# Token-tile attention and channel mix on one core: batch-wise pipeline on 64-token tiles, quarter-tile matmuls and a searched issue order

## The chip, the core, the metric

The kernel runs on one core of a Trainium2 chip. The metric is the device time of one execution in microseconds (us). Executions of one kernel differ (those of before beside the change took 107.15 to 110.02 us), so every run carries a state: "fast", or "slow" when it took over 1.5% more than the fastest of its kernel. Verdicts use fast runs alone. A median that is quoted is over all runs. A ratio is the mean time of one kernel's fast runs over the mean of the other's fast runs of the same rounds on the same chip, so it is not quite the ratio of the medians; the interval beside it covers 95%.

The engines are called as in the profile: PE is TensorE's matmul (PEld its weight load), DVE is VectorE, ACT is ScalarE, POOL is GpSimd, SP is SyncE.

## The reference

```python
# q, k, v: (4 batches, 4 heads, 1088 tokens, 32); S1, S2: (8, 32); all float32
def phi(x):                                   # 64 features for every token and head
    a = einsum('rd,bhsd->bhsr', S1, x)
    b = einsum('rd,bhsd->bhsr', S2, x)
    return einsum('bhsi,bhsj->bhsij', a, b).reshape(*x.shape[:-1], 64)
q_p, k_p = phi(q), phi(k)
kv  = einsum('bhsf,bhsd->bhfd', k_p, v)       # sum over all tokens of a batch
z   = k_p.sum(axis=2)
x   = (q_p @ kv) / (q_p @ z + 1e-6)           # then heads side by side: (4, 1088, 128)
# channel mix, d_ff = 1024
x_prev = x shifted by one token
xk = mu_k * x + (1 - mu_k) * x_prev
xr = mu_r * x + (1 - mu_r) * x_prev
out = sigmoid(xr @ w_r) * (maximum(xk @ w_k, 0) ** 2 @ w_v)
```

Denominators can come close to zero, so the attention half has to stay in float32. The channel mix (the "MLP" below) is done in bf16.

## The kernel before

It works on two batches at a time. A tile is 128 rows: 64 tokens of one batch and 64 of the other. k and q arrive partly head-major and partly token-major; the token-major half is turned by TensorE. In its trace each float32 matmul of the program stands as two passes (the 34 matmuls of the k projection, L198, as 68 records), and each pass as two instructions on TensorE, a weight load and a matmul (1,375 and 1,365 records in all).

```python
    def k_proj(half, gi):                     # per tile one matmul on the full array: 128 rows x 64 columns
        ...
            nc.tensor.matmul(p[:, t * 64:t * 64 + 64], kT[half][:, t0 + t, :], SW[:, 0, :, :2, :], skip_group_check=True)

    def k_acc(half, gi):                      # already in quarter tiles: 64 rows x 64 columns each
        ...
                    nc.tensor.matmul(kv[hp:hp + 64, b2, (h // 2) * 64:(h // 2) * 64 + 64],
                                     f[rows, t - t0, h].rearrange("p i j -> p (i j)"),
                                     _ap(rhs, [[(H - h) * NT * D, 2], [1, D]]), ...
                                     tile_position=(64 * b2, hp))

    def q_proj(g):                            # per tile two half-width matmuls, 96 columns each
        ...
                nc.tensor.matmul(p[64 * b2:64 * b2 + 64, t * 96:t * 96 + 96], qT[half][:, T, 64 * b2:64 * b2 + 64],
                                 SW[:, 2 * half + b2].rearrange("p h x r -> p (h x r)"), ...
                                 tile_position=(0, 64 * b2))

    def mm1(g, cp):                           # first MLP matmul of a group of tokens
        ...
    # loads: k0, v0, k1, q0, v1, q1 on three queues, and on GpSimd the weights only behind the second v pair:
    nc.gpsimd.tensor_copy(warm[:], tok["v1"][:R, 0, 0, :1])
    nc.gpsimd.dma_start(mu_k[:], moe_mu_k.rearrange("d -> d ()"))
    nc.gpsimd.dma_start(wk[:, :, :2 * P], moe_w_k.rearrange("p (c f) -> p c f", c=4))
```

The order in which tasks are issued is worked out by a small list scheduler with keys in the program. Zero matmuls ("fillers", 128x512) keep TensorE busy at the start: 19 of them, 7.6 us of busy time before 10.4 us (L84).

## Time and profile before

| | before |
|---|---|
| median, beside the change | 108.06 us (107.15 to 110.02, 4 runs) |
| profiled span | 107.7 us |
| first and last MLP matmul (mm1) | 52.1 and 102.5 us |
| instructions on TensorE (matmuls and weight loads) | about 2,750 |

The profile of before fell in a slow run (109.86 us, mean granted clock 0.95).

These are lines of the page of the kernel before. "busy us (share) xinstructions" comes first; then the span in 40 slices of 2.7 us, one digit each, in tenths; the queue that brings instructions; and the shares of the chain that ended last.

```profile
PE 95.0 (88%) x1365; PEld 71.6 (66%) x1375; DVE 77.8 (72%) x160; ACT 70.3 (65%) x124; POOL 10.6 (10%) x33
...
PE   5999990598789999976999999999999999999850
...
DVE  3275690123549796949999998599997997878770
ACT  0500410830293533767699999989999998999940
...
PEclk9999999679955699999999999999999999999999
...
q8 instruction: 11, 0.18, 0.7%
...
PE 50%; DMA 19%; ACT 13%; issue 5%; POOL 4%; DVE 3%; SPq 3%; ACTq 0%; POOLq 0%
```

The second half of the span is full on three engines; the first half is not. The table of stretches of the same kernel gives the figures (stretch, its length, then busy us of each engine with the instructions, the granted clock, the DMA share and GB/s), and the view of the mm1 line shows where the dense part begins (minimum/median/maximum duration, first and last start).

```profile
0.00:30.00 30.00, 23.75 (x368) 17.22 (x368) 13.78 (x35) 7.45 (x17) 8.30 (x21) 0.94 0.89 236
30.00:52.00 22.00, 20.31 (x411) 17.52 (x413) 17.21 (x37) 12.44 (x30) 2.31 (x13) 0.85 0.12 14
52.00:102.00 50.00, 49.03 (x568) 35.73 (x577) 44.71 (x85) 48.84 (x75) 0.00 (x0) 1.00 0.11 38
...
L398 PE MATMUL h<-XK,wk x62: 269/379/390, 52.1 to 102.5; 128*128 128x512 bf16 x54, 128*128 128x256 bf16 x8
```

### The profile page before, as it was taken

What the parts mean: (1) busy time and instruction counts of PE and PEld (TensorE: products, weight loads), DVE (VectorE), ACT (ScalarE), POOL (GpSimd) and SP (SyncE); (2) the same over time, 40 slices, a digit from 0 to 9 for tenths busy, and PEclk for the clock granted to TensorE, in tenths of its full rate; (3) what the DMA queues carried; (4) which work ended last, traced back from release to release, by engine and by line L of the source; (5) the groups of instructions that cost most, each with busy time, mean ns of one, the idle gap of its engine ahead of it and who ended that gap; (6) DMA issues with size and microseconds to landing.
All of it is one profiled execution on the core that took longest, in us unless ns stands there. A gap on an engine that the chain in (4) does not pass through costs nothing.

```text
span 107.7 us, 3217 instructions
## 1 busy us (share of the span) xinstructions
PE 95.0 (88%) x1365; PEld 71.6 (66%) x1375; DVE 77.8 (72%) x160; ACT 70.3 (65%) x124; POOL 10.6 (10%) x33
## 2 busy tenths in 40 slices
PE   5999990598789999976999999999999999999850
PEld 2445990487679889754667687776866776677720
DVE  3275690123549796949999998599997997878770
ACT  0500410830293533767699999989999998999940
POOL 7050000007790000000000000000000000000000
PEclk9999999679955699999999999999999999999999
DMA  0999999994990000000000000200202002122221
GB/s 10 343 293 366 279 280 287 209 272 159 127 98 0 0 6 6 3 6 0 3 0 6 0 0 0 97 6 0 97 6 97 0 8 90 30 73 97 97 100 53
DMA packets 6157, 9.70 MB, mean 90 GB/s; under 512 B 1520, under 2 KB 2416, under 8 KB 6144
## 3 DMA queue, kind: packets, MB, share of 16 engines
q1 hardware_dynamic: 3360, 6.13, 18.9%
q0 software_dynamic: 1952, 1.71, 8.7%
q10 hardware_dynamic: 832, 1.67, 4.9%
q8 instruction: 11, 0.18, 0.7%
q14 instruction: 2, 0.02, 0.1%
HBM read 7.80 MB, written 2.23 MB: 93 GB/s over the span
## 4 chain that ended last, share of the span: by engine, by line
PE 50%; DMA 19%; ACT 13%; issue 5%; POOL 4%; DVE 3%; SPq 3%; ACTq 0%; POOLq 0%
DMA tok_v_67<-in_v_dram 19%; PE o L419 10%; PE h L398 8%; PE xps L361 8%; PE qtp L323 7%; PE abwp L294 7%; PE tp L187 3%; PE kv L227 3%; PE abp L198 2%; SPq L71 2%; ACT r L435 1%; ACT PP_179 L379 1%; DVE osb L440 1%; ACT k_1507 L404 1%; PE rps L427 1%
## 5 line engine op out<-in xcount | busy, mean ns | idle before, releaser
L398 PE MATMUL h<-XK,wk 128*128 128x512 bf16 (+1 forms) x62 | 17.6, 366 | 0.2
L206 DVE TENSOR_TENSOR kp<-ab 128x1024 f32<-128x1024 f32 (+1 forms) x10 | 10.4, 1060 | 6.5 <-ACT ab L168 6.5
L187 PE MATMUL tp<-ident,tall 128*128 128x128 f32 x34 | 6.9, 340 | 4.1 <-ACT tall L182 4.1
L323 PE MATMUL qtp<-ident,qp 128*128 128x128 f32 x68 | 9.4, 275 | 1.1 <-ACT abw L168 1.0
L206 DVE TENSOR_TENSOR qp<-abw,an 128x1024 f32<-128x1024 f32 (+1 forms) x9 | 10.3, 1154 | 0.0
L168 ACT COPY qpT<-qtp 128x512 f32<-128x512 f32 x15 | 8.3, 601 | 2.4 <-PE qtp L323 2.3
L361 PE MATMUL xps<-qpT,kvbd 128*64 128x256 f32 (+3 forms) x80 | 9.3, 358 | 0.5 <-ACT qpT L168 0.5
L84 PE MATMUL zps<-zero 128*128 128x512 bf16 x19 | 7.6, 578 | 1.3 <-POOL zero L79 1.3
L323 PEld LDWEIGHTS qtp<-ident,qp 128*128 128x128 f32 x68 | 7.4, 142 | 1.6 <-ACT abw L168 1.2
L168 ACT COPY ab<-abp 128x256 f32<-128x256 f32 (+1 forms) x8 | 2.8, 352 | 8.8 <-PE abp L198 8.7
L187 PEld LDWEIGHTS tp<-ident,tall 128*128 128x128 f32 x34 | 4.7, 172 | 4.9 <-ACT tall L182 4.3
L398 PEld LDWEIGHTS <-wk 128*128 128x128 bf16 x72 | 5.8, 98 | 2.5 <-issue 1.0
L361 PEld LDWEIGHTS xps<-qpT,kvbd 128*64 128x64 f32 x80 | 4.5, 136 | 3.2 <-ACT qpT L168 0.7
L198 PE MATMUL abp<-SW,kT_160 128*128 128x64 f32 x34 | 5.5, 304 | 1.0 <-issue 1.0
L440 DVE TENSOR_TENSOR osb<-o,r 128x512 f32<-128x512 f32 (+1 forms) x9 | 5.9, 655 | 0.5 <-PE o L419 0.5
L198 PEld LDWEIGHTS abp<-SW,kT_160 128*128 128x128 f32 x34 | 5.1, 225 | 1.6 <-issue 1.6
L182 ACT COPY tall<-tok_k_68 128x512 f32<-128x512 f32 (+1 forms) x5 | 2.7, 556 | 5.1 <-DMA tok_k_68<-in_k_dram 5.1
L227 PE MATMUL kv<-tok_v_66,kp 64*64 64x64 f32 x272 | 5.9, 244 | 0.0
L84 PEld LDWEIGHTS <-zero 128*128 128x128 bf16 x19 | 2.4, 135 | 5.3 <-issue 3.6
L227 PEld LDWEIGHTS kv<-tok_v_66,kp 64*64 64x64 f32 x272 | 5.2, 155 | 0.8 <-DVE kp L206 0.3
L435 ACT ACTIVATE r<-rps 128x512 f32<-128x512 f32 (+1 forms) x9 | 5.5, 610 | 0.0
L168 ACT COPY abw<-abwp 128x384 f32<-128x384 f32 x6 | 2.9, 482 | 3.4 <-PE abwp L294 3.4
(246 smaller groups left out, 220.2 us busy)
## 6 DMA issues: line engine op xcount, KB each, us to landing
out_dram<-osb SPq DMA_DIRECT2D x7, 256.0 KB, 2.0
hd_k_70<-in_k_dram SPq DMA_DIRECT2D x1, 544.0 KB, 4.0
hd_k_71<-in_k_dram ACTq DMA_DIRECT2D x1, 544.0 KB, 6.0
tok_v_66<-in_v_dram SPq DMA_DIRECT2D x1, 544.0 KB, 8.6
tok_v_66<-in_v_dram ACTq DMA_DIRECT2D x1, 544.0 KB, 9.3
tok_k_68<-in_k_dram SPq DMA_DIRECT2D x1, 544.0 KB, 14.5
tok_k_68<-in_k_dram ACTq DMA_DIRECT2D x1, 544.0 KB, 16.5
tok_q_69<-in_q_dram SPq DMA_DIRECT2D x1, 544.0 KB
```

Source lines behind the costliest of these rows:

```text
L84: nc.tensor.matmul(zps[:, 0, :], zero[:, :P], zero[:], skip_group_check=True)
L168: nc.scalar.copy(o, i)
L187: nc.tensor.transpose(tp[:, t * P:t * P + P], tall[x, t0][:, t].rearrange("p h d -> p (h d)"), ident[:])
L198: nc.tensor.matmul(p[:, t * 64:t * 64 + 64], kT[half][:, t0 + t, :], SW[:, 0, :, :2, :], skip_group_check=True)
L206: nc.vector.tensor_mul(o, _ap(a_, list(a_.ap[1:]) + [[0, R]]), _ap(b_, list(b_.ap[1:3]) + [[0, R]] + [b_.ap[3]]))
L227: nc.tensor.matmul(kv[hp:hp + 64, b2, (h // 2) * 64:(h // 2) * 64 + 64], f[rows, t - t0, h].rearrange("p i j -> p (i j)"), _ap(rhs, [[(H - ...
L294: nc.tensor.matmul(p[64 * b2:64 * b2 + 64, t * 96:t * 96 + 96], qT[half][:, T, 64 * b2:64 * b2 + 64], SW[:, 2 * half + b2].rearrange("p h ...
L323: nc.tensor.transpose(p[:, t * P:t * P + P], qp[g][:, t, 2 * pair:2 * pair + 2].rearrange("p h i j -> p (h i j)"), ident[:])
L361: nc.tensor.matmul(o[64 * pair:64 * pair + 64], kvbd[:, 2 * half + b2, pair, :], qpT[g, pair][:].rearrange("p t (b s) -> p t b s", b=2)[:, ...
L398: nc.tensor.matmul(h[:, c, :n * P], wk[:, cp, c * P:c * P + P], XK[:, 4 * g:4 * g + n, :].rearrange("p t s -> p (t s)"))
L419: nc.tensor.matmul(bank["o", g][:, t * P:t * P + P], k2[:, c, t * P:t * P + P], wv[:, 2 * cp + c, :], start=(cp == 0 and c == 0 and t == 0 ...
L440: nc.vector.tensor_mul(o[:, :n].rearrange("p t f -> p (t f)"), bank.pop(("o", g))[:, :n * P], rs[g][:, :n * P])
```

## The change

The intent is to start the dense part earlier. Each batch gets its own chain on tiles of 64 tokens, all loads go on one queue in batch order at full width, VectorE makes all token transposes, TensorE does the projections in quarter tiles, any of its eight PSUM tiles ("banks") can serve any task, and the whole issue order with banks was searched beforehand and stands in the program as a string. Cut to its core:

```diff
-    NTT = 2 * NT                             # 34 tiles of two batches
+    SL = 64
+    NTT = B * NT                             # 68 tiles of 64 tokens
+    banks = [psum.tile([P, 512], F32, name=f"bank{i}", tag=f"bank{i}") for i in range(8)]
...
+    load_v(0)
+    load_kq("q", 0)
+    for b in range(1, B):
+        load_kq("k", b)
+        load_v(b)
+        load_kq("q", b)
...
-    nc.gpsimd.tensor_copy(warm[:], tok["v1"][:R, 0, 0, :1])
+    by_head(mu_k[:], moe_mu_k, ("d -> d ()",))       # weights regrouped by head, in pieces
+    ...
+    by_head(wr_f[:], moe_w_r, ("d f -> d f",))
...
+    def k_proj(b, t0, t1):                           # and q_proj alike with 24 columns, 4 x 17 matmuls a batch
+        for t in range(t0, t1):
+            for y in range(2):
+                rows = slice(64 * y, 64 * y + 64)
+                for x in range(2):
+                    nc.tensor.matmul(bank("ab", b, t0, y)[64 * x:64 * x + 64, (t - t0) * 16:(t - t0) * 16 + 16],
+                                     kqT["k", b][rows, t, :], SW[rows, 0, x, :2, :],
+                                     skip_group_check=True, tile_position=(64 * y, 64 * x))
...
-    tasks = {}                                       # list scheduler with keys
-    ...
+    ORDER = """
+        tk.0.0.0 tk.0.1.0 kpj.0.0@01 tk.0.0.9 tk.0.1.9 kpj.0.9@23 kab.0.0.0:DVE kab.0.9.1:ACT kab.0.0.1:DVE
+        ...                                          # name.arguments:engine@banks, all tasks
+    """
```

In the task names below, `kpj` is the k projection, `kacc` the k accumulation, `q1` the q projection, `num` the numerator; a number says which batch.

## The prediction

> **What bounds the kernel now.** The table of stretches shows two regimes. From 52 to 102 us three engines are nearly full: PE 49.0 of 50, ACT 48.8, DVE 44.7. Before 52 us they are not: DVE 31.0 of 52, ACT 19.9, much PE time is zero matmuls, and the granted clock is 0.50 from 30 to 35 us. The first MLP matmul starts at 52.1 us. The chain of waits says why: 19% of the span is the second v pair (3.9 to 24.5 us), with the weight loads queued behind it, and the k/q phase takes two batches at a time.
>
> **Costs, from the chain and the groups.** Real PE work: k projection 68 passes x 105 ns = 7.1 us; k accumulation 544 x 17 ns = 9.3; q projection 136 x 51 ns = 6.9; 34 token transposes x 110 ns = 3.7; 68 feature transposes 7.5; numerator 8.6; mm1 68 x 216 ns = 14.7; mm2 17; gate 3.9. Sum 79 us.
>
> - PE: token transposes vanish (-3.7). Each projection becomes 272 quarter-tile matmuls, 544 passes; quarter-tile passes cost 17 ns here (64 in 1.09 us), so 9.2 us each: +4.4. [...] PE stays about 79 us: quarter tiles are not the gain.
> - ACT: records overlap (1024-wide relus start 0.92 us apart, 512-wide evictions 0.46), so relu by single banks is free. Regroup copies (-5) and transpose evictions (-4) go, five squares come (+4.6). About 67 us.
> - DVE: all k and q transposes come here (16 of 544 columns, about 0.6 us each, +6), fewer denominators (-2), more feature-transpose evictions (+4), fewer squares (-3). About 80 us.
> - DMA: same bytes in batch order; the first batch needs 1.6 MB, 6 us at the measured 280 GB/s. Weights no longer wait for v.
>
> Total work hardly changes; the change is worth what it does to the first 52 us. DVE starts on batch 0 at about 7 us and can run on; the first MLP matmul should move from 52 to about 30 us.
>
> **Estimate.** PE: real start 8 us + 79 + tail 2.5 = 89.5. DVE: 7 + 76 + 2.5 = 85.5. [...] the dense stretch of before loses 2 to 10%; add 5 us. Half-clock time in the thin front: 2 us. Span 97; the reported time is 1 to 2 us above it. Predicted **99 us**, range **93 to 105.5**. Chances: faster 0.90, same 0.07, slower 0.03.
>
> **What would show it.** First MLP matmul near 30 us; DVE over 80% busy from 10 us on; ACT below 72 us; projection passes 13 to 20 ns; loads landing in batch order, the last near 27 us; weights by 20 us; PE group sum near 79 us; no stretch after 30 us with all engines idle.
>
> **What would make it wrong.** Projection passes at 25 ns or more (+9 us PE); row-tiled feature transposes not overlapping their weight loads (110 ns each, +7.5 us); [...] a fixed order on wrong assumed durations, so in-order queues block each other; one load queue slower than two; strided 512 B output rows landing late.

Carrying the 17 ns of a 64-column pass over to 16 and 24 columns: an estimate; the result bears it out (14.6 ns a pass for 16 and for 24 columns, 14.8 for 64, in full-rate bursts). Two more figures are estimates: the 0.6 us of a 544-column transpose (before took 0.42 us for 256 columns and 0.44 for 288, L175; a line through the two gives about 0.57; the change took 0.72) and the 2 us for half-clock time, for which the text gives nothing beyond the 0.50 granted from 30 to 35 us in the profile of before.

## The result, and the profile after

| | before | after |
|---|---|---|
| median | 108.06 us | 117.76 us (117.21 to 120.13, 4 runs) |
| ratio of fast runs | | 1.091 [1.076, 1.106] |
| instructions on TensorE | about 2,750 | about 4,550 |

The profile that came with the result fell in a slow run (120.13 us, mean granted clock 0.82). The same kernel was therefore run once more as experiment e0, and that profile, of a fast run (115.40 us, clock 0.94), is the one compared with before. The two clock figures can't be compared: the trace of e0 holds no clock record before 31.15 us, and the page and the mean count time without a record as full clock. First the page of the profile on record (slow):

```profile
PE 98.7 (83%) x2266; PEld 76.4 (65%) x2266; DVE 80.6 (68%) x163; ACT 68.6 (58%) x167; POOL 16.1 (14%) x44
...
q8 instruction: 18, 0.29, 1.1%
...
PE 64%; issue 10%; ACT 10%; DVE 8%; DMA 3%; SPq 1%; POOL 0%; DVEq 0%; POOLq 0%
```

And of the fast run of the same kernel (e0), the answers to the lines of before: page, stretches, and the mm1 line.

```profile
PE 99.2 (87%) x2261; PEld 75.7 (67%) x2266; DVE 80.6 (71%) x163; ACT 68.7 (60%) x167; POOL 16.1 (14%) x44
...
PE   5999867499979999995899999999999996998910
...
PEclk9999999999995579999656999999999999999999
...
q8 instruction: 17, 0.28, 1.0%
...
0.00:30.00 30.00, 25.01 (x622) 20.38 (x626) 14.74 (x42) 4.23 (x14) 15.26 (x32) 1.00 0.91 245
30.00:46.20 16.20, 15.56 (x548) 12.64 (x543) 11.73 (x23) 7.29 (x23) 0.79 (x13) 0.79 0.02 5
46.20:106.00 59.80, 56.42 (x1070) 40.66 (x1075) 51.52 (x93) 55.24 (x126) 0.00 (x0) 0.94 0.11 29
...
L389 PE MATMUL bank<-XK,wk x67: 269/379/423, 46.3 to 105.5; 128*128 128x512 bf16 x59, 128*128 128x256 bf16 x8
```

Total ACT and DVE work is what was predicted (68.7 and 80.6 us). The first MLP matmul came only 5.8 us earlier than before (46.3 against 52.1), not 22 us. And the dense part then takes longer, 59.2 us between first and last mm1 against 50.4 (50.5 in b1, from 49.7 to 100.2), as more of the attention of later batches now runs inside it (it is 56.3 us in e5 and e7 below, with some 1,630 instructions fewer to fetch). A gain of a few us in front and a loss of 8.8 us behind is the result in outline: the plan pays only if the front becomes short.

What fills the front? The timeline of e0 on PE (start, length, line, what, count, and in brackets idle time just before with what ended it) shows gaps put down to "issue", that is to nothing that the profile knows:

```profile
8.23 3.83 PE L204 MATMUL bank<-SW,kqT 64*64 64x16 f32 x136
12.40 2.19 PE L226 MATMUL bank<-vt,kp 64*64 64x64 f32 x68 [0.34 <-issue]
15.45 2.08 PE L226 MATMUL bank<-vt,kp 64*64 64x64 f32 x67 [0.85 <-issue]
...
17.32 1.83 PE L204 MATMUL bank<-SW,kqT 64*64 64x16 f32 x56
21.37 2.32 PE L204 MATMUL bank<-SW,kqT 64*64 64x16 f32 x76 [2.21 <-issue]
```

No semaphore ends these gaps, and they cut a burst in the middle of one task. Counting the instructions on TensorE in the records shows where: at numbers 448, 704, 1472 and 2752, which lie multiples of 256 apart. Between them the packets of the instruction queue land, one of 16 KiB each. The table is worked out from the records of e0 ("crossed" is when TensorE began the first instruction behind the boundary before; the fetch times are those of the packet):

```text
boundary  boundary before crossed   packet        longest gap between instructions at the boundary
   448         10.2                 13.0-14.0     1.17 us
   704         15.4                 19.1-20.1     2.48
   960         21.4                 23.0-24.5     0.05
  1216         26.1                 27.0-27.9     0.08
  1472         29.6                 30.6-31.5     0.85
  1728         33.0                 34.1-35.0     0.99 (behind a numerator; it ends 3.8 us after the packet)
```

By these records a block of 256 instructions is fetched one ahead (its packet starts 0.9 to 3.7 us after the boundary before was crossed), and it lands 3.2 to 4.7 us after the boundary before was crossed while the large loads run, and 1.8 to 2.0 us after it later on. TensorE does not go on at once: at each of the four stalls it resumed 1.3 to 1.5 us after the packet had landed (1.2 to 1.6 us in all runs together), which ties the stalls to the packets. Counted below as stalls are the gaps of 0.6 us and more at a boundary that end so. Before 60 us they sum to 5.9 us here, and to 1.3 in the kernel before.

A second thing is in the same lines. The first burst took 3.56 us from its first to its last start for 136 passes, 26 ns each, where the like burst of the q projection late in the kernel takes 1.97 us, 14.6 ns. In the first 31 us the array worked at about half its later rate. The clock row of the page reads full there only because no record exists: the first one, at 31.15 us, grants full clock, and at that moment the spacing of the passes falls from 25 to 14 ns.

### The profile page after: what moved, and what is told of

Read it like the earlier page. It is cut to its first block, busy times and chain, and to the rows that moved or that the text cites. A ratio compares the mean times of both kernels' runs of the same rounds, so it can differ in the third digit from the quotient of the medians.

```text
span 118.3 us, 5107 instructions
## 1 busy us (share of the span) xinstructions
PE 98.7 (83%) x2266; PEld 76.4 (65%) x2266; DVE 80.6 (68%) x163; ACT 68.6 (58%) x167; POOL 16.1 (14%) x44
## 4 chain that ended last, share of the span: by engine, by line
PE 64%; issue 10%; ACT 10%; DVE 8%; DMA 3%; SPq 1%; POOL 0%; DVEq 0%; POOLq 0%
PE bank_70 L226 6%; PE bank_67 L289 3%; PE bank_66 L226 3%; PE bank_66 L411 3%; PE bank_70 L204 3%; DMA out_dram<-osb 3%; PE bank_68 L358 3%; PE bank_66 L81 3%; PE bank_67 L204 2%; PE bank_69 L411 2%; PE bank_70 L389 2%; PE bank_72 L289 2%; PE bank_73 L204 2%; PE bank_72 L358 2%; DVE qp L187 2%
## 5 line engine op out<-in xcount | busy, mean ns | idle before, releaser
L187 DVE TENSOR_TENSOR kp<-ab 128x1152 f32<-128x1152 f32 (+1 forms) x8 | 10.0, 1286 | 1.2 <-ACT ab L182 1.2
L187 DVE TENSOR_TENSOR qp<-abw,an 128x1024 f32<-128x1024 f32 (+7 forms) x12 | 10.4, 908 | 0.1
L289 PE MATMUL bank_67<-SW,kqT 64*64 64x24 f32 x104 | 4.6, 236 | 2.5 <-issue 2.3
L289 PEld LDWEIGHTS bank_67<-SW,kqT 64*64 64x64 f32 x104 | 4.4, 164 | 3.5 <-issue 2.3
L289 PEld LDWEIGHTS bank_72<-SW,kqT 64*64 64x64 f32 x168 | 6.0, 152 | 0.8 <-ACT k_1485 L396 0.8
L226 PE MATMUL bank_70<-vt_91,kp 64*64 64x64 f32 x68 | 3.7, 281 | 3.3 <-issue 3.3
L289 PE MATMUL bank_72<-SW,kqT 64*64 64x24 f32 x168 | 6.2, 226 | 0.0
L204 PE MATMUL bank_73<-SW,kqT 64*64 64x16 f32 x68 | 4.1, 262 | 2.2 <-issue 2.2
L389 PE MATMUL bank_70<-XK,wk 128*128 128x512 bf16 x13 | 5.0, 381 | 1.1 <-DVE XK L378 1.1
L226 PEld LDWEIGHTS bank_70<-vt_91,kp 64*64 64x64 f32 x68 | 3.3, 191 | 3.6 <-issue 3.6
L204 PE MATMUL bank_67<-SW,kqT 64*64 64x16 f32 x104 | 4.6, 229 | 1.2 <-issue 1.2
L204 PEld LDWEIGHTS bank_73<-SW,kqT 64*64 64x64 f32 x68 | 4.0, 222 | 2.3 <-issue 2.3
L81 PE MATMUL bank_66<-zero 128*128 128x512 bf16 x12 | 4.2, 510 | 1.3 <-POOL zero L77 1.3
L389 PE MATMUL bank_73<-XK,wk 128*128 128x512 bf16 (+1 forms) x14 | 5.2, 371 | 0.0
L204 PEld LDWEIGHTS bank_67<-SW,kqT 64*64 64x64 f32 x104 | 4.3, 167 | 1.3 <-issue 1.3
L289 PE MATMUL bank_69<-SW,kqT 64*64 64x24 f32 x104 | 4.5, 236 | 0.0
L289 PEld LDWEIGHTS bank_69<-SW,kqT 64*64 64x64 f32 x104 | 4.1, 164 | 0.4 <-DVE pw_188 L303 0.4
L204 PE MATMUL bank_68<-SW,kqT 64*64 64x16 f32 x100 | 4.3, 227 | 0.0
```

The source lines that it names most:

```text
L81: nc.tensor.matmul(banks[i][:], zero[:, :P], zero[:], skip_group_check=True)
L187: nc.vector.tensor_mul(o, _ap(a_, list(a_.ap[1:]) + [[0, R]]), _ap(b_, list(b_.ap[1:3]) + [[0, R]] + [b_.ap[3]]))
L204: nc.tensor.matmul(bank("ab", b, t0, y)[64 * x:64 * x + 64, (t - t0) * 16:(t - t0) * 16 + 16], kqT["k", b][rows, t, :], SW[rows, 0, x, :2, :],
L226: nc.tensor.matmul(bank("kv", b, x)[64 * y:64 * y + 64, :2 * D], kp[b][rows, t, y].rearrange("p i j -> p (i j)"), _ap(vt[b][rows, y, t, :] ...
L289: nc.tensor.matmul(bank("q", b, r0, y)[64 * x:64 * x + 64, (r - r0) * 24:(r - r0) * 24 + 24], kqT["q", b][rows, t, :], SW[rows, b, x].rear ...
L389: nc.tensor.matmul(bank("h", g, c)[:, :n], wk[:, c // 2, (c % 2) * P:(c % 2) * P + P], XK[:, 8 * g:8 * g + qn[g], :].rearrange("p t s -> p ...
```

## The experiments

Theory: TensorE gets its instructions too slowly for strings of tiny matmuls. Rivals: GpSimd holds the denominators up; the halved array time of single passes, not their number, is what helps; the array's half rate; the searched order. Times are medians; "before" is rerun beside each call (106.8 to 107.5 us).

### e0: the change again

No edit.

> The changed kernel again, unchanged, to have a profile of it at an undisturbed clock. Theory F (instruction supply): TensorE's instructions come in blocks of 256, [...] so the gaps of about 2.5 us at TensorE instructions 448, 704 and 960 are there again at full clock, with more such gaps at later multiples of 256, 8 to 15 us in all, and the time is 117 to 118 us. Rival C (clock): the profile on record had half clock from 11 to 45 us; with a full clock the first MLP matmul moves from 49 us to about 35 us and the time falls below 110 us.

Measured: 117.14 us, ratio 1.097 [1.086, 1.109] as recorded (the two runs marked fast, 115.40 and 116.41, are at about 1.085 of the fast runs beside them), profile fast. Its lines are above. The stalls sum to less than the 8 to 15 us expected. The rival of the clock was not tested by this run, since its front ran at half rate as well.

### e1 and e2: one pass, and one pass issued twice

The upper halves of the float32 operands are read as bf16, so the three small kinds of matmul take one pass (the count of instructions falls from 4,546 to 2,911, or by 1,635). Their outputs are wrong, which doesn't matter for the times.

```diff
+def _hi(ap):
+    return ap.bitcast(BF16)[..., 1::2]
-   nc.tensor.matmul(bank("ab", ...)[...], kqT["k", b][rows, t, :], SW[rows, 0, x, :2, :], ...)
+   for _ in range(1):     # e2: range(2)
+       nc.tensor.matmul(bank("ab", ...)[...], _hi(kqT["k", b][rows, t, :]), _hi(SW[...]), ...)
```

> Both projections and the k accumulation read only the upper 16 bits of each fp32 number (as bf16), so each matmul is one pass in place of two: about 1630 of TensorE's 4500 instructions go; nothing else changes. Results are less exact on purpose. Theory F: about 11 blocks are fetched in place of 18, the gaps in the first 30 us shrink from about 9 us to under 3 us, first MLP matmul near 35 us, time 100 to 106 us. Rival O (the searched order and the waits between the engines cost the time, not TensorE's instruction stream): within 3 us of the changed kernel, 114 us or more. Rival P (fp32 array time of the small passes): also faster, but then the next run is just as fast.

Measured: 109.99 us, ratio 1.031 [1.023, 1.038], 2,911 instructions on TensorE. The expected 100 to 106 us was missed.

> As the run before, but each of these matmuls is issued twice in a row (sums of k are doubled in numerator and denominator alike), so TensorE has the changed kernel's number of instructions again, with bf16 passes. Theory F: the gaps at multiples of 256 instructions are back and the time is 113 to 118 us, near the changed kernel. Rival P (fp32 array time): stays at the time of the run before plus at most 4 us.

Measured: 114.94 us, ratio 1.073 [1.064, 1.082], 4,543 instructions; stalls at boundaries sum to 16.8 us. The number of instructions is worth about 5 us here even with passes that are cheap (8 ns each at full rate in e5). But e1 is still slower than before. Its list of waits names what is left (engine, line, what it waited for: us in total, times, longest):

```profile
POOL wr_c L267 <- DMA wr_f<-in_moe_w_r_dram: 10.9, 1, 10.9
DVE den L313 <- POOL pw L279: 9.6, 1, 9.6
```

The change put twelve small memsets of GpSimd (`pw`, `XB` and `PP`, four each) behind its multiplication `wr_c`, which waits for the last piece of `w_r`, and the weights, now loaded in pieces by head, land only near 29 to 30 us. VectorE's first denominator waits for a memset that could have run at any time.

### e3: only batch 0 is loaded

```diff
-    for b in range(1, B):
-        load_kq("k", b); load_v(b); load_kq("q", b)
+    for b in range(1, B):
+        kq["k", b], kq["q", b], vt[b] = kq["k", 0], kq["q", 0], vt[0]
```

> Only batch 0 of q, k and v is loaded and used for all four batches (wrong results on purpose): from about 9 us on no bulk load competes with the instruction fetches. If bulk loads slow the fetches, the gaps of 2.5 us at instructions 448, 704 and 960 shrink to 1 to 1.5 us and the time falls by 3 to 5 us; if the fetch latency is what it is without them, the gaps stay above 2 us and the time stays within 2 us of the changed kernel. Rival D (late loads hold up the front): the DVE transposes of batches 1 to 3 start earlier by several us and the time falls by more than 5 us with the gaps unchanged.

Measured: 112.25 us (109.97 to 113.5; one fast run, so no ratio; the profile is of a slow one). Stalls at boundaries fall to 2.2 us in all. The packets show that the loads do hold up the fetches: here the first five land 1.8 to 2.5 us after the boundary before was crossed, where in e0 the first three took 3.2 to 4.7. How much of the time gained is due to that stays open, since the weights land earlier as well.

### e4, e5, b1: the memsets first

```diff
+    kvbd, pw, XB, PP: allocated and set here, ahead of the weight loads
     nc.gpsimd.tensor_copy(warm[:], kq["k", 0][:R, 0, 0, :1])
-    ... (the same memsets at their old places; pw, XB and PP behind wr_c and wr_p)
```

> The changed kernel with GpSimd's small memsets (kvbd, the epsilon columns pw, the zero columns of XB and PP) put ahead of the weight loads instead of behind wr_c, which waits for the gate weights until 29 us. Theory G: this gate is real (in the one-pass run the first denominator waited 9.6 us for it) but in the changed kernel it is hidden behind the instruction gaps (0.2 us of wait on it), so alone it gains 0 to 2 us: 115 to 117 us. Rival: it is the main cause; then 109 us or less.

Measured: 117.14 us, ratio 1.098 [1.089, 1.106]. Alone it is worth nothing.

> One pass and the early memsets together (results less exact on purpose). If instruction gaps and the memset gate are the two things that hold up the front, the first MLP matmul comes at 32 to 36 us and the time is 98 to 104 us, well below the one-pass run's 110. If 107 us or more, something else in the front or in the later stages costs the rest.

Measured: 101.83 us (99.67 to 102.08; one fast run, 99.67), first MLP matmul at 36.0 us. With fewer instructions to supply, moving the memsets is worth about 8 us by the medians (109.99 to 101.83), and 10 by the one fast run. The two causes lie one behind the other: the GpSimd wait is hidden as long as TensorE is late anyway.

> The kernel before with the same small memsets ahead of the weight loads. ACT waits 3.7 us for kvbd at 25 to 29 us there, in a stretch where TensorE also waits; if that wait is on the critical path the time falls by 2 to 4 us, if loads bound that stretch by less than 1 us.

Measured: 106.92 us, ratio 0.994 [0.984, 1.004]. The kernel before has nothing of it.

### e6: loads spread out

```diff
+        kq[x, b] = work.tile([P, 2, NT + 1, D], F32, name=f"{x}raw", tag=f"{x}raw", bufs=1)
-    all loads issued at the start
+    ORDER: "... tk.0.1.9 ld.k.1 ld.v.1 ... tk.1.1.0 ld.k.2 ..."     # a load once its buffer is free
```

> Exact results: early memsets, and the loads of batches 1 to 3 issued only when the transposes have read the batch before (one buffer for k and one for q), so that fewer loads are in flight while instruction blocks are fetched. If bulk loads stretch the fetches [...], the gaps at 448 and 704 shrink below 1.2 us each and the time is 109 to 113 us, as in the run with one batch loaded (112.3). If not, 115 us or more.

Counted from the crossing of the boundary before, packets landed after 1.8 to 2.5 us in e3 and 3.2 to 4.7 us under the loads of e0.

Measured: 116.47 us, ratio 1.089 [1.079, 1.099]. No help: gaps of 4.5 and 2.8 us appear (in a slow profile) at boundaries 960 and 1216 in place of the earlier ones, where the loads now run (276 to 309 GB/s from 20 to 28 us); there the packets land 6.5 and 4.7 us after the boundary before was crossed. Spreading the loads moved the stalls and did not remove them.

### e7 and e8: array time apart from the number of instructions

e1 and e5 cut the array time along with the instructions (the first burst of e5 took 0.89 us, that of e0 3.56). e7 keeps e5's 2,916 instructions and makes each single pass long, by repeating the moving operand to 240 or 256 columns; e8 keeps short passes and issues each twice, 4,548 instructions. Both have the memsets first. Their outputs are wrong, which doesn't matter for the times.

```diff
 # e7
-   ...[(t - t0) * 16:(t - t0) * 16 + 16], _hi(kqT["k", b][rows, t, :]), _hi(SW[...])
+   w = _hi(SW[...]); n = min(16, 32 - (t - t0))
+   ...[(t - t0) * 16:(t - t0) * 16 + 16 * n], _hi(kqT["k", b][rows, t, :]), _ap(w, [[0, n], list(w.ap[-1])])
```

> The one-pass kernel with the GpSimd memsets first (101.8 us), with every single pass of the projections and of the k accumulation widened to 240-256 columns by repeating the moving operand, so that TensorE's array works about as long as with two passes or longer while the number of its instructions stays near 2,910. Wrong on purpose. Theory (what was gained was instruction supply): at most 106 us, first MLP matmul by 38 us, no more than two stalls over 1 us at block boundaries in the first 50 us. Rival (what was gained was the halved array time of the passes): 112 us or more.

> The one-pass kernel with the GpSimd memsets first, with each of these single passes issued twice: about 4,550 instructions on TensorE again, the memsets still early, the arithmetic still wrong on purpose. Theory (instruction supply is the larger cause): 112 to 117 us, block stalls of 2 to 4 us back in the first 50 us, first MLP matmul at 44 us or later. Rival (the GpSimd gate was the larger cause and number of instructions matters little): 104 us or less.

Measured: e7 102.72 us, ratio 0.954 [0.947, 0.961]; e8 115.76 us, ratio 1.084 [1.078, 1.090], all its runs fast; its stalls at boundaries before 60 us sum to 16.7 us, the longest 4.2. The first bursts of e7 in the timeline on PE:

```profile
8.81 2.60 PE L218 MATMUL bank<-SW,kqT 64*64 64x256 bf16 x68
12.53 2.24 PE L241 MATMUL bank<-vt,kp 64*64 64x256 bf16 x68 [1.12 <-DVE kp L198]
14.95 2.08 PE L218 MATMUL bank<-SW,kqT 64*64 64x256 bf16 x68 [0.18 <-DVE kqT L207]
```

and of e8, followed by the six longest pieces of "issue" in its chain of waits (start, us):

```profile
8.82 1.78 PE L216 MATMUL bank<-SW,kqT 64*64 64x16 bf16 x136
11.96 0.79 PE L239 MATMUL bank<-vt,kp 64*64 64x64 bf16 x68 [1.37 <-DVE kp L198]
15.33 1.12 PE L239 MATMUL bank<-vt,kp 64*64 64x64 bf16 x67 [2.57 <-issue]
...
21.25 1.24 PE L216 MATMUL bank<-SW,kqT 64*64 64x16 bf16 x76 [4.00 <-issue]
...
12.76 2.57 issue
17.26 4.00 issue
24.54 2.36 issue
28.83 1.92 issue
32.65 1.84 issue
51.37 2.16 issue
```

This pair is the cleanest. In e8 the array itself works less on a burst than in e7 (1.61 us for the first k projection from first to last start, against 2.33), and yet the kernel is 13 us slower. What differs is 1,632 instructions, and the six pieces of "issue" make 14.85 us of the chain. The rival, array time, falls. The clock is no rival either: by the records e8's front ran at half clock from 13.5 to 44.2 us and e7's only from 20.2 to 23.6, but e5, with e7's count, ran its short passes at half rate until 31.2 us (13 ns each, 8 after that) and is as fast as e7.

e8 also gives the price of a block. Where TensorE stood at two boundaries in a row, the second stall ended 5.9 and 5.7 us after the first while the loads ran, and 3.9 and 3.7 us later on. The 128 passes of a block of the change take 1.9 us at 14.6 ns, and 3.3 us at 26 ns: supply is the slower of the two while loads run, and close to the half rate after them.

### e9: fewer matmuls, with a right result

The quarter tiles are merged in pairs. The projections contract over all 128 rows against weights padded with zeros; the accumulation computes both heads of a row half at once, 96 columns of which a part is not used. Two passes stay, 816 small matmuls become 408.

```diff
-    SW = const.tile([FD, B, 2, 3, R], F32)
+    SW = const.tile([FD, B, 2, 2, 3, R], F32)        # zero for the other half of the rows
 # k_proj (q_proj alike)
-   for y: for x: matmul(bank(..y)[64*x:.., 16 columns], kqT[rows, t, :], SW[rows, 0, x, :2, :], tile_position=(64 * y, 64 * x))
+   for x: matmul(bank(..i)[64*x:.., 32 columns], kqT[:, t, :], SW[:, 0, x, :, :2, :], tile_position=(0, 64 * x))
 # k_acc
-   for y: for x: matmul(bank(..x)[64*y:.., :64], kp[rows, t, y], v of head (x, y) and ones, tile_position=(64 * x, 64 * y))
+   for x: matmul(bank(..x)[:, :96], kp[rows, t], vt[b][rows, :, t, :], tile_position=(64 * x, 0))
```

> A version meant to be correct: the changed kernel with the memsets first, and with the quarter-tile matmuls merged in pairs: the projections contract over all 128 rows against zero-padded weights and write half-width column tiles, the k accumulation works in two row tiles with 128 feature columns and 96 moving columns. Two-pass fp32 stays, 816 small matmuls become 408, TensorE's instructions about 2,920 in place of 4,550; same issue order, same banks. Theory (instruction supply and GpSimd gate): 100 to 105 us, below both kernels, first MLP matmul at 35 to 38 us. Rival (two fp32 passes or the searched order set the time whatever the count): 113 us or more.

Measured: correct, 110.07 us (one fast run of 107.22, three slow of 109.58 to 110.68), 2,919 instructions, no stall at a boundary, first MLP matmul at 39.0 us. That is below 117 and misses the 100 to 105. The chain of waits of the fast run shows why (start, us, what):

```profile
9.34 2.65 PE bank L218 x68
12.00 0.90 issue
12.90 4.04 PE bank L239 x68
```

A merged projection burst costs what the quarter tiles cost at full rate (later ones 1.95 us for 68 passes against 1.97 for 136), but the merged accumulation takes 3.77 us where quarter tiles take 2.0: its passes are 56 ns long.

### e10, e11, e12: a new order

A search over issue orders used a sum with the pass times measured here and about 4 us for each block of 256 instructions (6 us while the loads run), as e8 had shown (3.7 to 3.9 and 5.7 to 5.9). e10 reorders e9; e11 reorders a mixed version (merged projections, accumulation in quarter tiles); e12 reorders the change itself with all its 4,550 instructions. All have the memsets first; otherwise only the ORDER string differs, and a line that lets the relus of a pair come in either order.

> Correct. The kernel with 408 merged matmuls and the memsets first, with a new issue order and banks, searched with the pass times measured here and with about 4 us for each block of 256 instructions on TensorE (6 us while the loads run). The search's own sum gives 95.7 us where it gives 102.0 for the old order that measured 105.4 in the profile, so 98 to 104 us is expected of the median, at least 5 us less than the same instructions in the old order. Rival (the order is not what is left; the longer k accumulation passes are): within 2 us of 110.

Measured: correct; 104.38 us in one fast run, 113.4 to 113.8 in three slow ones. The median, 113.49, misses the expected 98 to 104. The profile is of a slow run, with half clock on record from 7.7 to 35.0 us. The two groups are not explained: the mean clocks of the runs (0.997 for the fast one; 0.87, 0.87 and 0.99) do not separate them.

> Correct. Merged projections, but the k accumulation back in quarter tiles of 16 ns (544 instructions more, about 6.8 us less on TensorE's array than merged), again with a newly searched order (the search's sum gives 94.3 us). Theory: 97 to 103 us, level with or a little below the all-merged version in its new order, since two more blocks of instructions to fetch buy back the array time; stalls of 1 us at block boundaries return in some k accumulations. If instruction supply is worse than the 4 us per block put into the search: over 105 us.

Measured: correct, 104.08 us, ratio 0.971 [0.962, 0.981], stalls at boundaries 2.5 us. It is below both kernels, but 1 us above the expected 97 to 103; the verdict at the 2% line is unclear.

> Correct. The changed kernel with all its quarter-tile matmuls (4,550 TensorE instructions) and the memsets first, only the issue order and banks newly searched with the cost of instruction supply in the sum (104.1 us against 113.0 for its old order, which measured 113.6 to 115.1 in the profile). Theory (the old order queued 8.5 blocks of tiny matmuls ahead of the first MLP matmul, and mixing them with MLP work hides part of the fetches): 105 to 112 us. Rival (the count alone decides, no order can hide it): 114 us or more.

Measured: correct, 117.85 us, ratio 1.099 [1.089, 1.109]. The expectation missed, and the rival named the right number for a reason that the trace does not bear out: stalls at boundaries did fall, to 1.2 us. But the passes stayed at half rate until about 44 us. A numerator and two bursts of one kind in e12's timeline (profile of a slow run, clock 0.97):

```profile
34.17 1.98 PE L357 MATMUL bank<-qpT,kvbd 128*64 128x512 f32 x4 [0.83 <-DVE qpT L191]
36.08 3.83 PE L211 MATMUL bank<-SW,kqT 64*64 64x16 f32 x136
...
55.23 2.17 PE L211 MATMUL bank<-SW,kqT 64*64 64x16 f32 x136
```

Line L211 took 3.83 us at 36 us and 2.17 us at 55 us for the same 136 passes. The page of this profile gives clock 9 in every one of the slices from 34 to 40 us, but the trace has no clock record before 43.85 us, where full clock is granted. So a 9 ahead of the first record says nothing; the length of known passes does, and where records exist the two agree (in the profile on record 136 passes took 1.97 us at a granted clock of 1.0, from 6.84 us, and 3.81 us at 0.5, from 33.26 us).

### e13, e14, e15, e16: fillers against the half rate

Zero matmuls (128x512 bf16, two instructions) are added for TensorE, to see whether the array then runs at full rate and what that is worth. In e13 one stands before every second tile inside the early bursts of the change (72 in all); in e14 one before every third tile in four early tasks of e12, and 25 in its waits; in e15 18 in the waits of e11; in e16 38 before tasks of the change, none inside.

```diff
+    def filler(t):                                   # e13, e14, called inside k_proj, k_acc, q_proj
+        if fill[0] is not None and t % 2 == 0:       # e14: % 3
+            spin(fill[0], 1)
 # e15, e16: entries in ORDER
-  kp.0.0 kacc.0.0@45
+  kp.0.0 spin.8@4 kacc.0.0@45
```

> Correct. The changed kernel, its own order, memsets first (117.1 us), with 72 filler matmuls (zeros, 128x512, 0.216 us each at full rate, two instructions) put between every second tile of the quarter-tile work before the first MLP matmul. They cost 15.6 us of array time, in a stretch where the array waits or runs at half rate. If instruction supply alone sets the front: 112 to 118 us, passes at full rate but boundary stalls only partly gone, since 144 more instructions have to come. If the half rate of the array sets it: 106 us or less. If neither is helped: over 120 us.

> Correct. The newly ordered quarter-tile kernel (117.9 us, block stalls of about 4 us in all, passes at 1.8 times their length until 42 us), with 25 filler matmuls in the waits before 45 us and one in every third tile of four early tasks. If the half rate is what was left: passes at full rate from about 12 us, 106 to 111 us. If not: within 2 us of 117.9.

Measured: e13 145.88 us, e14 126.13 us, both correct. They answer nothing about the rate, since the tool was bad: in e13 a filler with two tiles took about 0.67 us where 0.22 and 0.23 us had been reckoned (216 ns from filler to filler at full rate, L81, and 16 passes at 14.6 ns), so each cost about twice its estimate.

> Correct. The mixed version in its new order (104.1 us, passes at half rate until 25 us), with 18 filler matmuls in the waits of TensorE before 32 us. If the half rate costs there too: 99 to 102 us. If not, the fillers are harmless or cost up to 1 us: 103.5 to 105.5 us.

Measured: correct, 102.94 us (101.25 to 103.95), ratio 0.948 [0.943, 0.954]: faster than before. The median lies between the two expected ranges. In its trace passes run at full rate from 7 us on, but for 28.8 to 32.2 us. The ratios of e11 and e15, 0.971 and 0.948, put the fillers at about 2%. The stretches and the mm1 line of e15:

```profile
0.00:30.00 30.00, 26.07 (x547) 18.77 (x552) 23.97 (x61) 8.55 (x25) 15.05 (x42) 0.98 0.92 246
30.00:34.00 4.00, 4.00 (x142) 2.39 (x142) 1.47 (x2) 1.47 (x3) 1.38 (x2) 0.73 0.01 4
34.00:93.00 59.00, 58.25 (x1049) 42.63 (x1046) 55.18 (x106) 56.24 (x137) 0.00 (x0) 1.00 0.12 31
...
L397 PE MATMUL bank<-XK,wk x68: 269/379/390, 34.2 to 92.1; 128*128 128x512 bf16 x60, 128*128 128x256 bf16 x8
```

DVE is busy 23.97 us of the first 30, against 14.74 in e0, and the dense part starts at 34.2 us.

> Correct. The changed kernel, its own order, memsets first (117.1 us), with 38 filler matmuls before tasks, none inside them: about 10 us with what entering and leaving them costs, most of it in waits. If instruction supply sets the front: passes at full rate (14 to 15 ns) from about 12 us, but 113 to 119 us, because 272 instructions at full rate take 2.0 us and then wait for their block, where at half rate they took 3.6 us and waited less. If the half rate was the main cause: 108 us or less.

Measured: correct, 120.00 us (118.19 to 122.9, one fast run), 1 us above the 113 to 119 expected if supply sets the front; first MLP matmul at 48.2 us. The timeline of e16 on PE:

```profile
10.36 1.12 PE L211 MATMUL bank<-SW,kqT 64*64 64x16 f32 x64
11.41 1.90 PE L81 MATMUL bank<-zero 128*128 128x512 bf16 x8
13.24 1.08 PE L233 MATMUL bank<-vt,kp 64*64 64x64 f32 x57
15.54 0.46 PE L233 MATMUL bank<-vt,kp 64*64 64x64 f32 x15 [1.22 <-issue]
...
18.53 0.87 PE L211 MATMUL bank<-SW,kqT 64*64 64x16 f32 x43
21.46 2.06 PE L211 MATMUL bank<-SW,kqT 64*64 64x16 f32 x93 [2.07 <-issue]
```

Passes run at full rate here until 22 us (64 in 0.92 us from first to last start), but then the array stands and waits for its block, and the front is as long as ever. It is not a wholly free comparison, as the fillers take about 6 us of the first 28, and by the clock record full rate ended at 22.3 us and came back at 32.6. It does show that full rate, got in this way and for this long, brings nothing as long as 4,600 instructions have to come.

## Why the prediction was wrong

The following table is worked out from the records: the time from first to last start of each of the first six bursts of small matmuls (k projection and accumulation of batches 0 and 1, q projection of batch 0, k projection of batch 2). The prediction's figure for them was 816 passes at 17 ns, 13.9 us.

```text
kernel  TensorE instr.  six bursts, us                          sum    median, us
e0        4,546         3.56  4.81  6.03  3.56  3.14  2.74      23.8   117.1
e8        4,548         1.61  4.25  6.02  4.34  3.92  3.80      23.9   115.8
e9        2,919         2.50  3.77  1.95  1.97  3.77  1.95      15.9   110.1
e7        2,916         2.33  1.97  1.82  2.36  3.20  1.80      13.5   102.7
e5        2,916         0.89  1.54  0.88  0.88  4.97  0.87      10.0   101.8
```

The first two rows belong together. Of e0's 23.8 us, 4.5 are stalls at boundaries; the passes take the rest, 19.3 us, where 816 at 14.6 ns would take 11.9. Of e8's 23.9 us, 13.7 are stalls. Passes of half the length leave the sum the same: what the array no longer takes, it waits.

Point by point:

- **What bounds the kernel before: right.** Two regimes, with the dense one beginning at 52 us.
- **Work of ACT and DVE: right.** About 67 and 80 us were predicted; 68.7 and 80.6 came out.
- **"PE stays about 79 us: quarter tiles are not the gain": right in the pass time at full rate, wrong as a time.** (The sum of 79 us itself was not measured.) At full rate a quarter-tile pass takes 14.6 ns, less than the 17 ns predicted. But the 17 ns had been read from 64 passes at a stretch, 128 instructions, which is half a block. The change strings 136 passes to a burst and burst to burst, 272 instructions each, and supply begins to count.
- **"The first MLP matmul should move from 52 to about 30 us": the step that failed.** It came at 46 to 50 us. Nearly all of the miss lies there: behind that matmul the prediction leaves 67 us of its span of 97, and e0 took 67.3 (46.3 to 113.6). The six bursts ahead of it took 23.8 us in place of 13.9. What was left out is the supply of instructions: TensorE's count rose from 2,758 to about 4,550 and the packets of its queue from 11 to 17, and about nine blocks of them (2,327 instructions in e0, against 1,572 in the kernel before) lie ahead of the first MLP matmul in the searched order. Keeping the array time and cutting the count (e7) gives 102.7 us, and cutting the array time and keeping the count (e8) gives 115.8. That is shown, with single passes; for the change's own double passes it is carried over. With the count cut and the memsets moved (e5) the first MLP matmul is at 36 us and the median at 101.8 us, inside the range of 93 to 105.5, though with a wrong result.
- **"Weights no longer wait for v" and "weights by 20 us": wrong, and a second cause, hidden behind the first.** `w_r` in four pieces landed near 29 us, and twelve memsets stood behind it on GpSimd. Alone they cost nothing (e4), once instructions come in time 8 us (e1 against e5).
- **"Half-clock time in the thin front: 2 us": too small, but not a cause of its own as far as shown.** Early bursts of the change run at 26 ns a pass, about 3.6 us each in place of 2.0; in the six bursts of e0 that makes 7.4 us. With the array at full rate until 22 us (e16) the time did not fall; with the stalls reduced (e12) it did not either. A burst of 272 instructions takes about 3.6 us at half rate, and at full rate 2.0 us plus a wait for its block. Two limits stand at nearly the same height, so lifting one shows little. That reading fits the runs. No run here lifts both at 4,550 instructions.
- **Listed risks.** Passes at 25 ns or more and a halved clock were listed, and both happened: 26 ns in the first burst of e0, and half clock on record from 10.8 to 45.0 us in the slow profile. The supply of instructions was not on the list, though the page of before showed its queue.

Open: what lets the array leave half rate (e9 left it at 10 us, e10 in its slow profile only at 35 us with the same instructions in another order); why e10 falls into two groups; what the change would take with the array at full rate through the whole front.

The change's plan itself holds. With about 1,050 instructions fewer on TensorE, memsets first, an order searched with the cost of supply in the sum, and fillers in the waits (e15), it is correct and takes 102.94 us, 5.2% less than before by the ratio.

## What to carry to other kernels

Before cutting matmuls into smaller tiles, count instructions, not only array time: here 272 instructions for 2 us of array work outran the fetch, which brought 256 in 3.7 to 5.9 us where TensorE had to wait for every block (e8). A pass time read from a burst shorter than one block did not hold for strings of blocks (17 ns predicted, 29 ns a pass over the six bursts of e0, stalls and half rate included), so look for gaps put down to "issue" that recur every 256 instructions, and merge tiles until the block lasts longer than its fetch. Before the clock row of a page is believed, look where its first record stands. And when a removed bottleneck gives back less than expected, look for a wait that had been hidden behind it: here a few memsets, issued on GpSimd behind a multiplication that waited 10.9 us for a late load (e1).
